# A block-sparse attention with a relu-squared layer on one core: SyncE's transfers wait for older ones from the third batch on, and one normalising changes places with two masks

## The chip, the core and the metric

The kernel runs on one core of a Trainium2 chip. Its time is the device time in microseconds of one execution; of several executions the median is given. The engines are TensorE (PE in the profile), VectorE (DVE), ScalarE (ACT), GpSimd (POOL) and SyncE (SP), which here only issues transfers. A core has 16 DMA engines, shared by all queues.

## The reference, cut to what matters

```python
batch, n_heads, seq, head_dim = 4, 8, 768, 64;  block = 32;  n_blocks = 24;  n_rand = 3
scores = (q @ k.T) / sqrt(64)                    # for each batch and head
mask = |blk_i - blk_j| <= 1  or  blk_i in (0, 23)  or  blk_j in (0, 23)
mask[rows of block qb, columns of block kb] = True   for kb in sampled_blocks[qb]
attn = softmax(where(mask, scores, -1e9))
x = (attn @ v) as [3072 tokens, 512]
out = relu(x @ w_in) ** 2 @ w_out                # w_in 512 x 2048, w_out 2048 x 512
```

Inputs and output are in float32; the kernel computes in bfloat16 with float32 sums.

## The kernel before, in words

The work is a list of small tasks, numbered in the order in which they are made, and a written-out order of them, `PROGRAM` (L1009). A word such as `V433` names the engine (V VectorE, P TensorE, A ScalarE, G GpSimd, S SyncE) and the task; `/2` behind a TensorE task is the PSUM buffer, one of four, that it takes. `run_program` (L96) goes through the words and emits each task. Every engine works off its own words in this order; between engines they wait for each other's data and buffers by semaphores. `HOLD` (L77) lets four gathers of GpSimd begin behind a named product.

A *unit* is a pair of heads of one batch: four units a batch, 16 in all. Batches 0 and 1 (units 0 to 7) are computed densely: scores of 256 queries against 256 keys at a time, `exp` on ScalarE (L364), a multiplication by the 0/1 mask on VectorE (`masks`, L371), the products with V (`values`, L376) and a normalising on VectorE (`normalize`, L410: a reciprocal, L414, and a multiplication, L417). The normalising reads the PSUM buffer in which the products with V were summed, and that buffer is free for other work when it is done.

Batches 2 and 3, the third and the fourth, (units 8 to 15) are computed sparsely, in six *visits* of four query blocks each. For a visit `k_gather` (L589) copies the sampled K blocks from the transposed K (`QKT`) into `KG`, on GpSimd or VectorE, and `v_gather` (L576) fetches the sampled V rows from a copy in DRAM into `VG`, with an indirect transfer of GpSimd or six small ones of SyncE; `v_window` (L547) fetches the neighbouring and the first and last V rows. The products with V come out of L660.

Around this run the transfers of SyncE, in the order of the S words: `load` (L151) brings a unit's q, k or v in float32 into SBUF (V at L155; Q and K of the third and fourth batch at L157, in rows of 512 bytes); a cast on GpSimd, VectorE or ScalarE; `transp_dma` (L318) turns the cast Q or K into `QKT` with a transposing transfer at L319; `v_store` (L539) writes V rows to DRAM for the gathers; `x_transp_dma` (L442) and `s_transp` (L672) transpose the normalised result into `xT`; `store` (L774) writes the output. SyncE works strictly in order: a transfer that has to wait for its data or its buffer holds all later ones.

The second layer, in tiles of 256 tokens, fills in between: `hidden` (x times w_in), `relu`, `square`, `output` (g times w_out), `out_copy`, `store`. Most matmuls are issued in pairs, for the two halves of the rows, by a helper at L209.

The place of the order that the change touches, around the end of the second batch, reads

```python
A903 P432 P906 P476/0 V418 P481/2 A477 S621 V412 V433 A482 V498 V541 G499 P914/1
V478 V483 P915 G503 P486/0 P419/2 ...
```

`P432` finishes the products with V of unit 7's last 256 queries, `V433` normalises them, `P914/1` (a `hidden` part) takes the PSUM buffer 1 that `P431/1` and `P432` had used. `V418` and `V412` are masks of unit 6, whose products are `P419` and `P420`. `P476` and `P481` are the first scores against gathered K blocks of the third batch; `V502`, ahead of all these V words, picks blocks with `k_gather`. `S435` transposes the normalised result of the second batch once all four units' are there.

Of the kernel before, what the change touches and what calls it, by code (L numbers as in the profile page):

```python
# [25 lines left out]
def kernel(  # L26
# [49 lines left out]
    AHEAD = {(2, 4, 9): 2, (3, 0, 1): 0}  # L76
    HOLD = {586: 976, 563: 977, 564: 978, 542: 956}  # L77
# [18 lines left out]
    def run_program(bufs):  # L96
# [81 lines left out]
    sy, sc_ = nc.sync, nc.scalar  # L178
# [772 lines left out]
    for us in [range(b * HP, (b + 1) * HP) for b in range(B)]:  # L951
        for u in us:
# [20 lines left out]
    for T in TILES:  # L973
# [34 lines left out]

    PROGRAM = """  # L1009
        V109 V153 V207 V332 V18 V19 V20 V28 V42 V53 V294 V29 A32 V35 P30/0 P36/1 V31 P0/2 V1 P2/3 P15/0 P33/2 G43 A3 V37 P100/0 V34  # L1010
        P84/1 G46 P104/3 G57 P88/2 V85 A101 V89 G54 P98/1 A105 P102/0 V99 P92/2 P47/3 P44/1 A103 V93 P9/2 A48 G41 P58/0 P94/2 P86/3
        A59 V45 P111/1 A87 V95 P113/0 P55/2 P106/3 V67 A112 A114 V56 G64 P68/1 P123/2 V107 P14/0 G74 V52 A69 P108 A124 G75 P115/1 G78
        S80 P90/0 V110 V91 P125/3 G63 A116 P121/2 P65/0 A122 P117/1 V66 G49 P82/0 A126 G70 P135/2 V118 P119 P131/3 G38 A136 V83 V60
        V120 P133/0 P61/2 V73 P127/1 V62 P174/2 A132 P50/3 A134 V128 A175 P171/0 P129 V51 V130 A172 P10/3 V176 P168/3 P11/1 P4/2
        P39/1 A169 V40 V173 P137/2 G22 P144/0 A145 P12/1 P5/1 V138 V170 P141/1 P139 P147/3 V140 A142 P71/0 P177/2 V146 A148 P158/1
        V72 V178 P781/0 V149 A159 P782 P179 V180 S251 G79 V160 P184/3 P783 V143 P784 G76 S252 A185 P187/1 P774/2 P775 P181/3 A188
        P776 P777 P161/1 V785 V189 P150/0 V186 A182 A778 V151 P788/3 A162 P155/2 P789 G786 P152 A156 V183 G780 P215/1 A216 V154 P790
        P212/0 V163 P791 V157 P190/2 A792 V787 P164/1 A213 V191 P795/3 G793 A779 V165 P796 S81 P209/0 G794 P192 P166 P797 V167 V193
        P798 A210 P824/1 V217 V214 S259 S260 V383 G77 P825 A799 P197/2 P194/0 P826 A198 G801 P827 P818/3 A195 V828 P819 G254 P226/2
        A800 P820 S255 V196 A227 P200/0 P812/1 V211 V264 P813 A201 S267 P243/2 P821 V256 S265 P814 A244 V228 P218/0 P815 V199 A822  # L1020
        P219 P802/2 A816 V220 S257 V202 P240/3 P221 P803 A241 V262 S261 P96/1 P804 A222 V97 A817 P237/3 V242 P223/0 P203/1 A238 S268
        V245 P805 S263 V272 A224 P229/3 P204 P806 A230 G266 S275 S276 P286/0 V225 A823 P807 S273 V231 A287 P808 V205 P232/3 A829 V270
        P206 P289/0 S271 P233 V239 V208 P809 A290 V234 V288 P296/1 S253 A810 P246/0 V291 S437 P235 P247 V236 A297 P299/2 V248 P830/3
        P831 A300 V280 P302/1 V278 P832 A303 P249 S279 P283/2 V250 P833 V298 A284 P852/0 V834 V434 P314/1 S277 P853 A315 S281 P846/2
        V304 P847 A835 V285 P311/3 P854 V258 P855 A312 V301 P848 S269 P849 V316 A856 P292/1 S21 V313 P864/3 A850 P293 P305/0 G282
        V295 P865 A857 P308/2 G851 S454 P306 S436 A309 P866 V307 P353/1 P867 A354 P326/0 V868 P858/2 G439 P859 A327 P320/1 P860 V274
        A321 P323/3 S438 V310 P836/0 S444 A324 V355 S460 P861 V322 P347/1 S445 P837 V496 A862 V328 V325 G441 P317/3 A348 P350/2 P318
        P838 S811 V319 A351 V349 P329/1 A869 P334/3 V352 P330 P839 V331 A335 V23 P356/2 G443 A863 P340/1 P840 S333 A341 P841 P362/3
        P357 G447 P842 A363 P337/1 P843 S452 A338 G459 S442 P870/3 G449 A844 P359/1 P871 S446 A360 V345 V342 V358 S440 V339 P374/0
        P872 A375 V336 P365/1 S450 P377/2 V361 P873 A366 V364 P343/0 S462 A378 V367 P371/1 P344 S845 P874 A372 S448 V346 V376 P368/2  # L1030
        P398/0 V373 P369 A399 P875 V379 S461 V370 P380/1 V470 S453 P401/0 P381 A402 P385/2 V382 P876 V400 A386 S384 P391/0 P16/1 P877
        V451 A392 V403 P404/1 P886/2 V878 A405 P887 P388/0 P425/1 A389 V406 P24/3 P888 V27 V25 A426 P889 P880/0 A890 P881 G463 P428/1
        P882 A429 G467 P883 V427 V26 S613 P407/2 G465 S631 A884 P408 S468 S469 A891 P892/1 P893 P422/3 G455 S464 V396 V409 P926/0
        V457 P927 P894 S456 P928 V390 A423 P929 P895 S466 A885 V424 P413/2 V387 A930 G471 V393 P898/3 A414 V896 P899 S458 P394/0 A931
        P900 V430 P395 S615 P416/1 A417 A897 P932/2 V397 P901 S605 P933 V902 V539 G473 P410/0 P431/1 P934 S614 A411 P935 V415 S472
        P904/3 A936 V502 P905 A903 P432 P906 P476/0 V418 P481/2 A477 S621 V412 V433 A482 V498 V541 G499 P914/1 V478 V483 P915 G503
        P486/0 P419/2 A487 P907 A937 P916 P491/0 P917 A492 P420 A918 P479/0 P908 V421 A480 S435 V488 P489/2 P920/1 V545 A490 P474/0
        G546 P909 A475 P484/2 V493 P910 S501 G616 A485 P911 G500 A919 P494/0 V912 G626 S913 P921 V519 V495 S544 P507/2 P7/3 P922 A508
        P513/3 P923 A514 G636 P948/2 G620 V582 P949 A924 V515 P510/0 P504/3 P950 V509 S623 A511 P951 G523 A505 P954/1 V952 P553/0
        A925 P955 S606 P938/3 V512 S622 P556/2 V506 P939 S879 A557 G524 P940 A554 S497 P956 G542 G543 P547/2 P957 A548 P941 V958 S617  # L1040
        P516/0 V549 V558 P525/2 V584 P550/1 V517 P942 A526 G588 A959 P943 S518 P944 A953 S522 P528/2 A551 P966/0 P967 A529 G520 V552
        S627 P945 V555 V530 G618 P960/1 A946 P968 P531/2 P961 A532 G608 P969 P962 S630 V970 G624 P534/3 P963 S609 A535 P559/2 G521
        V665 V533 A971 V589 S629 G566 V562 A964 P994/0 P995 S619 P988/3 V560 P989 G965 P996 V610 P990 P593/1 P997 A594 S561 P991 V536
        P972/2 A998 V992 G628 G585 P1000/1 S607 A999 P973 V527 V567 S611 S587 P590/0 P1001 A591 P974 P1002 S625 P1003 P537/3 A1004
        P982/0 V667 V538 A993 P983 G632 G612 P975 V634 A1005 S540 S633 P984 V595 P596/1 P976 G586 P568/3 P985 S635 A597 P977 G563
        V708 V986 A569 S565 P599/1 V598 P978 G564 S637 A600 S638 V601 P574/3 S947 P979 A575 P1022/0 A987 V980 P1023 P571/1 P1028/3
        A572 V592 S981 P1029 P1024 V573 P1025 V642 P577/2 P1030 P602/1 A578 G668 A1026 P1006/2 V639 V603 G640 A1027 P643/0 P1007 V570
        S604 G671 A644 P1008 V576 S641 V579 P655/1 P1031 A656 P1034/0 A1032 P1035 P1009 P648/1 P1036 A649 P1037 P580/3 A1038 P1010
        V710 V581 A1033 P645/1 P658/3 V672 P1011 S583 A659 P1012 A646 P650/0 P1016/3 V647 A651 P660/1 P1017 A661 P653/0 P1013 V662
        A654 V657 V652 P1018 V692 A1014 P1019 G693 P663/1 V751 A1020 S1015 A1039 P682/0 G1021 V664 P679/2 P1050/3 A680 S670 P1051  # L1050
        P1056/1 A683 P676/2 G669 V681 P1052 P1053 P1062/0 S666 A677 P1057 V1054 P1063 P1058 P673/2 P1064 A674 P1059 P1040/3 A1055
        V1060 P1065 P1068/2 V684 A1061 P1069 V675 P694/1 V678 P1041 A1066 V714 P1070 A695 P685/0 G715 A1067 P1071 V688 V753 V686
        P700/1 P1042 A1072 G1073 S687 P1043 A701 G689 P722/0 P697/2 P1044 A723 S712 V702 P703/1 P1045 A704 P716/0 A698 P1046 V735
        P725/1 A717 P1047 G736 P1090/2 A1048 V696 P1091 P1084/0 G690 A726 P1085 P719/3 P1092 A720 G757 S713 P1074/1 P1093 V758 P1086
# [42 lines left out]
```

## Time and profile before

| | |
|---|---|
| median of 3 runs | 258.28 us (256.19 to 260.79) |
| the profiled execution's own time | 257.4 us |
| its span in the profile | 255.6 us |
| granted clock of TensorE | 1.000 |
| DMA: bytes, mean rate over the span | 47.08 MB, 184 GB/s |
| of these on q1, SyncE's queue | 37.61 MB, 65.2% of the 16 engines' time |
| on q0, GpSimd's queue | 8.25 MB, 16.2% |

How to read it: the profile lists every instruction of one execution with its engine and its line in the kernel. A group's row names line, engine, operation, the buffers written and read (out<-in), how many there were and their busy time. In the timeline a row has start, length and, in square brackets, the engine's idle time before it with what ended it; "issue" stands for an end that no semaphore of the program explains. SPq is SyncE, which is never "busy": its rows tell how long it took to issue transfers. A row of the view by window has start:end, length, and then for each engine, in the order PE, PEld (weight loads of TensorE), DVE, ACT, POOL, the busy time and the number of instructions in brackets; then the granted clock, the DMA engines' share and the rate in GB/s. A row of a DMA queue has packets, MB and their time as a share of 16 engines over the window. A row of the view of waits has who waits for whom, the total in us, how often, and the longest.

### The profile page before, as it was taken

Reading aid. Unit: us, or ns where it says so; the run is one execution under the profiler, and the core shown is the slowest. Engines: PE = TensorE matmul, PEld = TensorE weight load, DVE = VectorE, ACT = ScalarE, POOL = GpSimd, SP = SyncE. Lnnn points to the kernel's source line nnn. Section 1 sums busy time; section 2 is a strip of 40 time slices with the busy share of each in tenths; the row PEclk is TensorE's granted clock in tenths of the full one; section 3 lists DMA queues with packets and bytes.
Section 4 is the critical chain, followed back from the end, with each engine's and each line's share of the span. In section 5 each row is a group of like instructions: output and inputs, shape, how many; then the busy total and the mean of one; then the engine's idle time right before and its main releaser. Section 6 shows DMA issues by size and latency. Waiting matters only on the chain.

```text
span 255.6 us, 12045 instructions
## 1 busy us (share of the span) xinstructions
PE 242.8 (95%) x5265; PEld 182.0 (71%) x5265; DVE 165.6 (65%) x386; ACT 184.8 (72%) x216; POOL 99.0 (39%) x200
## 2 busy tenths in 40 slices
PE   7998999999999989969999899899999999999994
PEld 4776888669865668857967676666975775776774
DVE  7779987799787878764654666526465478642300
ACT  3899999999998798948648476758697647225241
POOL 2674253010544015167466844144427406150020
PEclk9999999999999999999999999999999999999999
DMA  6999999999899999997799999983525654342022
GB/s 197 371 265 212 197 308 130 251 216 230 224 291 188 248 169 263 142 269 142 225 278 148 185 232 204 291 221 82 159 44 88 158 152 112 94 128 82 3 85 85
DMA packets 63540, 47.08 MB, mean 184 GB/s; under 512 B 31487, under 2 KB 58496, under 8 KB 63488
## 3 DMA queue, kind: packets, MB, share of 16 engines
q1 hardware_dynamic: 58352, 37.61, 65.2%
q0 software_dynamic: 4448, 8.25, 16.2%
q8 instruction: 41, 0.67, 1.2%
q10 hardware_dynamic: 688, 0.46, 0.6%
q14 instruction: 11, 0.09, 0.1%
HBM read 35.51 MB, written 7.91 MB: 170 GB/s over the span
## 4 chain that ended last, share of the span: by engine, by line
PE 81%; DVE 8%; DMA 5%; issue 2%; ACT 1%; DVEq 0%; POOL 0%; SPq 0%; ACTq 0%; POOLq 0%
PE X L209 73%; PE X L660 5%; DMA VG<-rows,idx 3%; DVE pT L371 2%; PE X L402 2%; DMA QKT<-qc 2%; ACT pT L364 1%; DVE r L716 1%; DVE VG L286 1%; DVE xq L417 1%; PE X L312 1%; DVE KG L604 0%; DVE VB L129 0%; DVE oh L238 0%; DVE rs L414 0%
## 5 line engine op out<-in xcount | busy, mean ns | idle before, releaser
L209 PE MATMUL X<-xT,w_in_sb 64*128 64x256 bf16 x1536 | 99.7, 269 | 3.1 <-DVE XS L417 2.0
L209 PE MATMUL X<-w_out_sb,g 64*128 64x512 bf16 (+3 forms) x960 | 94.5, 333 | 0.0
L209 PEld LDWEIGHTS <-w_in_sb 64*128 64x128 bf16 x1536 | 73.5, 94 | 16.0 <-issue 4.1
L364 ACT ACTIVATE pT<-X 128x1024 bf16<-128x1024 f32 x72 | 70.5, 1034 | 5.5 <-PE X L209 4.4
L630 ACT ACTIVATE pT<-X 128x768 bf16<-128x768 f32 (+1 forms) x56 | 41.5, 766 | 28.7 <-PE X L209 27.1
L209 PEld LDWEIGHTS <-g 64*128 64x128 bf16 x960 | 40.3, 94 | 26.2
L725 ACT ACTIVATE g<-r 128x1024 bf16<-128x1024 f32 (+1 forms) x43 | 39.6, 936 | 11.8 <-DVE r L716 11.7
L371 DVE TENSOR_TENSOR pT<-pT,VG 128x1024 bf16<-128x1024 bf16 x60 | 41.1, 720 | 2.4 <-ACT pT L364 0.9
L716 DVE TENSOR_SCALAR r<-X 128x1024 f32<-128x1024 f32 x21 | 25.7, 1223 | 24.6 <-PE X L209 23.0
L727 POOL TENSOR_TENSOR g<-r 128x512 bf16<-128x512 f32 (+1 forms) x16 | 21.2, 1338 | 50.0 <-DVE r L716 26.7
L714 ACT ACTIVATE r<-X 128x1024 f32<-128x1024 f32 x27 | 28.4, 1064 | 10.8 <-PE X L209 10.7
L637 DVE TENSOR_TENSOR pT<-pT,MKS 128x768 bf16<-128x768 bf16 (+1 forms) x48 | 27.4, 602 | 12.1 <-ACT pT L630 11.2
L209 PE MATMUL X<-QKT 64*128 64x256 bf16 (+1 forms) x384 | 32.8, 254 | 1.6 <-issue 0.8
L583 POOL DMA_INDIRECT VG<-rows,idx x20 | 20.4, 1019 | 25.7 <-PE X L209 12.2
L209 PEld LDWEIGHTS <-QKT 64*128 64x128 bf16 x384 | 17.4, 97 | 7.0 <-issue 2.4
L129 POOL CAST qc<-ks 128x384 bf16<-128x384 f32 (+1 forms) x18 | 10.0, 582 | 27.0 <-DMA ks<-in_k_dram 17.9
L129 POOL CAST VB<-vs 128x768 bf16<-128x768 f32 x10 | 9.7, 972 | 24.8 <-DMA vs<-in_v_dram 23.5
L209 PEld LDWEIGHTS <-pT 64*128 64x128 bf16 x768 | 15.7, 94 | 3.0 <-PE X L209 0.2
L209 PE MATMUL X<-VB,pT 64*128 64x65 bf16 x768 | 17.2, 190 | 0.1
L209 PEld LDWEIGHTS <-KG 64*128 64x128 bf16 x528 | 13.3, 95 | 4.4 <-POOL KG L604 0.3
L660 PEld LDWEIGHTS <-pT 128*64 128x64 bf16 x624 | 11.8, 111 | 5.2 <-issue 4.8
L209 PE MATMUL X<-QKT,KG 64*128 64x64 bf16 x528 | 15.0, 190 | 0.0
(107 smaller groups left out, 201.5 us busy)
## 6 DMA issues: line engine op xcount, KB each, us to landing
vs<-in_v_dram SPq DMA_DIRECT2D x14, 384.0 KB
ks<-in_k_dram SPq DMA_DIRECT2D x13, 384.0 KB
qs<-in_q_dram SPq DMA_DIRECT2D x12, 384.0 KB
out_dram<-ys SPq DMA_DIRECT2D x9, 512.0 KB
VG<-rows SPq DMA_DIRECT2D x20, 132.0 KB
w_in_sb<-in_moe_w_in_dram POOLq DMA_DIRECT2D x2, 1024.0 KB, 11.7
w_out_sb<-in_moe_w_out_dram POOLq DMA_DIRECT2D x4, 512.0 KB, 14.5
rows<-VB SPq DMA_DIRECT2D x4, 396.0 KB
```

The costliest lines, as they stand in the source:

```text
L129: (V if e == "DVE" else G).tensor_copy(out=out, in_=in_)
L209: last = nc.tensor.matmul(out(r ^ crossed), lhsT(r ^ crossed, rows), rhs(r ^ crossed, rows), skip_group_check=True, **kw)
L364: A.activation(out=pT[:, :, 0:n], in_=stile.pop(a)[:, :, 0:n], func=AF.Exp, scale=scale)
L371: V.tensor_tensor(out=pT, in0=pT, in1=m[:, None].broadcast_to([P, 2, len(cs), w]), op=AOP.mult)
L583: G.indirect_dma_start(out=to[0:RS * HB], out_offset=None, in_=pairs, in_offset=bass.IndirectOffsetOnAxis(ap=idx[0:RS * HB, g - 1:g], axis=0))
L630: A.activation(out=pT[:, :, 0:n], in_=stile.pop((u, v, gs))[:, :, 0:n], func=AF.Exp, scale=scale)
L637: V.tensor_tensor(out=pT, in0=pT, in1=m[:, None].broadcast_to([P, 2, n]), op=AOP.mult)
L660: nc.tensor.matmul(po[i * D:(i + 1) * D, h, a * VW:(a + 1) * VW], pts[g][:, h, c * D:(c + 1) * D], val, start=a == 0 and c == 0, stop=c == ...
L714: A.activation(out=to, in_=src, func=AF.Relu)
L716: V.tensor_scalar(out=to, in0=src, scalar1=0.0, scalar2=None, op0=AOP.max)
L725: A.activation(out=g, in_=r, func=AF.Square)
L727: (G if e == "POOL" else V).tensor_mul(out=g, in0=r, in1=r)
```

## The change

Two things change. First, SyncE's transfers go through a small class, `Paced`. It keeps for each transfer a name and a cost, the number of rows times (1000 + bytes in a row). From the first S word whose task belongs to the third batch or to anything made after it (`S437`, the load of unit 8's K, and with it all later S words, whatever their batch), each transfer first counts back from the youngest one sent: as long as the sum of costs stays within 1,900,000 they may be under way. If there is an older one that is not yet known to have landed, SyncE gets an instruction ahead of the transfer that does nothing but wait for the landing of the youngest of those. Transfers of GpSimd and ScalarE are not counted and do not wait. Second, in `PROGRAM` the word `V433` moves from behind `V412` to ahead of `V418`; all other words keep their order (the diff breaks the lines anew).

```diff
+    ROW_COST, UNDER_WAY = 1000, 1900000
...
             held_by[0] = passed.get(HOLD.get(int(i)))
+            sy.on = sy.on or (word[0] == 'S' and t in third)
             t.fn(names[word[0]])
...
-    sy, sc_ = nc.sync, nc.scalar
+    class Paced:
+        def __init__(self):
+            self.sent, self.landed, self.on = [], 0, False
+
+        def dma_start(self, out, in_, **kw):
+            row = (D * 2 if kw else in_.shape[-1]) * (4 if in_.dtype == F32 else 2)
+            cost = math.prod(in_.shape) // (D * 2 if kw else in_.shape[-1]) * (ROW_COST + row)
+            under_way, k = 0, len(self.sent)
+            while k > self.landed and under_way + self.sent[k - 1][1] <= UNDER_WAY:
+                k -= 1
+                under_way += self.sent[k][1]
+            if self.on and k > self.landed:
+                tc.add_manual_dep(nc.sync.nop().ins, self.sent[k - 1][0], SYNC, reason="little is under way when the next transfer begins")
+                self.landed = k
+            i = nc.sync.dma_start(out=out, in_=in_, **kw)
+            self.sent.append((i.ins.name, cost))
+            return i
+
+    sy, sc_ = Paced(), nc.scalar
...
     for us in [range(b * HP, (b + 1) * HP) for b in range(B)]:
+        if us[0] == SB * HP:
+            first = len(tasks)
         for u in us:
             prepare(u)
...
+    third = set(tasks[first:])
     PROGRAM = """
...
-        A903 P432 P906 P476/0 V418 P481/2 A477 S621 V412 V433 A482 V498
+        A903 P432 P906 P476/0 V433 V418 P481/2 A477 S621 V412 A482 V498
```

More of the change, by code (lines that the diff above doesn't have):

```diff
@@ L1013 @@
[L1013 to L1048, printed above, removed]
@@ L1061 @@
[L1061 to L1064 removed]
+        V109 V153 V207 V332 V18 V19 V20 V28 V42 V53 V294 V29 A32 V35 P30/0 P36/1 V31 P0/2 V1 P2/3 P15/0 P33/2 G43 A3 V37
@@ new lines @@
+        P100/0 V34 P84/1 G46 P104/3 G57 P88/2 V85 A101 V89 G54 P98/1 A105 P102/0 V99 P92/2 P47/3 P44/1 A103 V93 P9/2 A48 G41
+        P58/0 P94/2 P86/3 A59 V45 P111/1 A87 V95 P113/0 P55/2 P106/3 V67 A112 A114 V56 G64 P68/1 P123/2 V107 P14/0 G74 V52
+        A69 P108 A124 G75 P115/1 G78 S80 P90/0 V110 V91 P125/3 G63 A116 P121/2 P65/0 A122 P117/1 V66 G49 P82/0 A126 G70
+        P135/2 V118 P119 P131/3 G38 A136 V83 V60 V120 P133/0 P61/2 V73 P127/1 V62 P174/2 A132 P50/3 A134 V128 A175 P171/0
+        P129 V51 V130 A172 P10/3 V176 P168/3 P11/1 P4/2 P39/1 A169 V40 V173 P137/2 G22 P144/0 A145 P12/1 P5/1 V138 V170
@@ new lines @@
+        P200/0 P812/1 V211 V264 P813 A201 S267 P243/2 P821 V256 S265 P814 A244 V228 P218/0 P815 V199 A822 P219 P802/2 A816
+        V220 S257 V202 P240/3 P221 P803 A241 V262 S261 P96/1 P804 A222 V97 A817 P237/3 V242 P223/0 P203/1 A238 S268 V245
+        P805 S263 V272 A224 P229/3 P204 P806 A230 G266 S275 S276 P286/0 V225 A823 P807 S273 V231 A287 P808 V205 P232/3 A829
+        V270 P206 P289/0 S271 P233 V239 V208 P809 A290 V234 V288 P296/1 S253 A810 P246/0 V291 S437 P235 P247 V236 A297
+        P299/2 V248 P830/3 P831 A300 V280 P302/1 V278 P832 A303 P249 S279 P283/2 V250 P833 V298 A284 P852/0 V834 V434 P314/1
@@ new lines @@
+        P927 P894 S456 P928 V390 A423 P929 P895 S466 A885 V424 P413/2 V387 A930 G471 V393 P898/3 A414 V896 P899 S458 P394/0
+        A931 P900 V430 P395 S615 P416/1 A417 A897 P932/2 V397 P901 S605 P933 V902 V539 G473 P410/0 P431/1 P934 S614 A411
+        P935 V415 S472 P904/3 A936 V502 P905 A903 P432 P906 P476/0 V433 V418 P481/2 A477 S621 V412 A482 V498 V541 G499
+        P914/1 V478 V483 P915 G503 P486/0 P419/2 A487 P907 A937 P916 P491/0 P917 A492 P420 A918 P479/0 P908 V421 A480 S435
+        V488 P489/2 P920/1 V545 A490 P474/0 G546 P909 A475 P484/2 V493 P910 S501 G616 A485 P911 G500 A919 P494/0 V912 G626
@@ new lines @@
+        S913 P921 V519 V495 S544 P507/2 P7/3 P922 A508 P513/3 P923 A514 G636 P948/2 G620 V582 P949 A924 V515 P510/0 P504/3
+        P950 V509 S623 A511 P951 G523 A505 P954/1 V952 P553/0 A925 P955 S606 P938/3 V512 S622 P556/2 V506 P939 S879 A557
+        G524 P940 A554 S497 P956 G542 G543 P547/2 P957 A548 P941 V958 S617 P516/0 V549 V558 P525/2 V584 P550/1 V517 P942
+        A526 G588 A959 P943 S518 P944 A953 S522 P528/2 A551 P966/0 P967 A529 G520 V552 S627 P945 V555 V530 G618 P960/1 A946
+        P968 P531/2 P961 A532 G608 P969 P962 S630 V970 G624 P534/3 P963 S609 A535 P559/2 G521 V665 V533 A971 V589 S629 G566
@@ new lines @@
+        V562 A964 P994/0 P995 S619 P988/3 V560 P989 G965 P996 V610 P990 P593/1 P997 A594 S561 P991 V536 P972/2 A998 V992
+        G628 G585 P1000/1 S607 A999 P973 V527 V567 S611 S587 P590/0 P1001 A591 P974 P1002 S625 P1003 P537/3 A1004 P982/0
+        V667 V538 A993 P983 G632 G612 P975 V634 A1005 S540 S633 P984 V595 P596/1 P976 G586 P568/3 P985 S635 A597 P977 G563
+        V708 V986 A569 S565 P599/1 V598 P978 G564 S637 A600 S638 V601 P574/3 S947 P979 A575 P1022/0 A987 V980 P1023 P571/1
+        P1028/3 A572 V592 S981 P1029 P1024 V573 P1025 V642 P577/2 P1030 P602/1 A578 G668 A1026 P1006/2 V639 V603 G640 A1027
@@ new lines @@
+        P643/0 P1007 V570 S604 G671 A644 P1008 V576 S641 V579 P655/1 P1031 A656 P1034/0 A1032 P1035 P1009 P648/1 P1036 A649
+        P1037 P580/3 A1038 P1010 V710 V581 A1033 P645/1 P658/3 V672 P1011 S583 A659 P1012 A646 P650/0 P1016/3 V647 A651
+        P660/1 P1017 A661 P653/0 P1013 V662 A654 V657 V652 P1018 V692 A1014 P1019 G693 P663/1 V751 A1020 S1015 A1039 P682/0
+        G1021 V664 P679/2 P1050/3 A680 S670 P1051 P1056/1 A683 P676/2 G669 V681 P1052 P1053 P1062/0 S666 A677 P1057 V1054
+        P1063 P1058 P673/2 P1064 A674 P1059 P1040/3 A1055 V1060 P1065 P1068/2 V684 A1061 P1069 V675 P694/1 V678 P1041 A1066
@@ new lines @@
+        V714 P1070 A695 P685/0 G715 A1067 P1071 V688 V753 V686 P700/1 P1042 A1072 G1073 S687 P1043 A701 G689 P722/0 P697/2
+        P1044 A723 S712 V702 P703/1 P1045 A704 P716/0 A698 P1046 V735 P725/1 A717 P1047 G736 P1090/2 A1048 V696 P1091
+        P1084/0 G690 A726 P1085 P719/3 P1092 A720 G757 S713 P1074/1 P1093 V758 P1086 G711 A1094 P1096/3 P1097 P1087 A1095
+        P1098 S691 V1088 P1075 P1076 V705 S1049 V718 P1099 V721 P1102/2 V699 P1103 S754 V1100 P1077 P706/0 V727 A1101 P743/3
+        V707 P1078 A744 V724 P1104 S709 P762/0 P1105 A763 P728/3 A1089 P768/0 V731 S734 P1079 V729 A1106 P1080 V764 S730
@@ new lines @@
+        A769 G1107 P1081 P765/3 P737/2 P1108/0 A766 S756 V770 G732 V1082 A738 P1109 P746/3 P1110 G733 V739 V745 P1111 V767
+        A747 G755 P1132/2 P1118/1 P740/3 P1119 A741 P1133 P1120 V742 P759/3 P1121 V748 A760 P1112 V1122 P749/3 V761 P1134
+        V750 P1135 P1139/1 S752 V1136 P771/3 P1113 A1137 G1138 V772 P1140 S773 G1124 P1125/2 P1126 P1141 G1123 S1083 P1142
+        P1127 A1143 P1128 P1114 V1129 G1144 P1115 A1131 P1156/3 A1116 P1157 P1146/1 A1145 S1117 P1158 A1130 P1163/2 P1159
+        P1164 V1160 P1147 P1148 A1162 A1161 P1177/0 P1165 P1178 P1170/3 P1171 P1179 P1180 P1149 V1181 P1172 P1173 P1166
@@ L1065 @@
+        A1174 P1150 V1167 P1151 A1169 G1168 P1152 A1183 P1153 A1176 G1175 A1182 P1184/0 A1154 P1185 P1186 S1155 P1187
+        P1194/3 P1195 P1188 P1189 P1190 P1196 P1197 P1191 P1198 A1192 P1199 P1200 P1201 S1193 P1214/2 P1215 P1216 A1202
+        P1217 P1204/1 P1205 P1206 S1203 P1218 P1219 P1207 P1220 P1221 P1208 P1209 A1222 P1210 P1211 P8/0 S1223 P6/3 P13/2
+        P17/0 V1212 S1213
     """
```

34 lines of the change are left out of this document (15 added, 19 removed).

## The prediction

> **What bounds the kernel now.** I read the page first, then who the TensorE waits for, then the chain that ended last, then the queue of SyncE and the DMA queues one by one.
>
> ```profile
> PE 242.8 (95%) x5265; PEld 182.0 (71%) x5265; DVE 165.6 (65%) x386; ACT 184.8 (72%) x216; POOL 99.0 (39%) x200
> q8 instruction: 41, 0.67, 1.2%
> ```
>
> TensorE is busy for 95% of the span, so the kernel is bound by its matmuls, and a change to queues and order can only win idle time of that engine. How much there is, and where, the next two views say: busy time by stage, and TensorE's waits from 56 us, about where the new waits begin, to 175 us.
>
> ```profile
> 56.00:170.00 114.00, 108.49 (x2467) 82.03 (x2462) 79.69 (x195) 89.29 (x101) 48.29 (x101) 1.00 1.07 219
> 170.00:255.60 85.60, 82.02 (x1774) 59.47 (x1770) 39.39 (x89) 46.36 (x60) 28.82 (x55) 1.00 0.39 100
> PE X L209 <- DVE XS L417: 2.0, 1, 2.0
> PE X L209 <- issue: 1.8, 2, 1.0
> PE X L660 <- issue: 1.3, 2, 1.1
> ```
>
> In the first stage the DMA engines are full (share 1.07) and TensorE idles 114.00 - 108.49 = 5.51 us. In the second the DMA share is 0.39, and the 3.6 us of idle time are mostly the last stores. Of the 5.51 us, 2.0 + 1.8 + 1.3 = 5.1 us are in five waits: one for a normalising (L417) and four in which TensorE waits for nothing that the program shows ("issue"). So 5.1 us, 2.0% of the run, is all that can be won.
>
> The "issue" waits have a pattern. Here are three of them in the timeline, then the instructions between them (the third and the fifth column's counts, matmuls and weight loads), then how many were left when a fetch of instructions began on queue q8 (the packets below).
>
> ```profile
> 93.62 0.28 PE L209 MATMUL X<-QKT 64*128 64x256 bf16 x2 [0.81 <-issue]
> 146.04 0.28 PE L209 MATMUL X<-xT,w_in_sb 64*128 64x256 bf16 x1 [0.96 <-issue]
> 165.28 0.38 PE L660 MATMUL X<-VG,pT 128*64 128x65 bf16 x11 [1.12 <-issue]
> 93.60:104.51 10.91, 10.72 (x256) 9.18 (x255) 9.24 (x19) 9.71 (x11) 4.06 (x7) 1.00 1.10 240
> 104.51:146.02 41.51, 38.40 (x892) 29.50 (x892) 23.61 (x58) 28.12 (x35) 26.30 (x73) 1.00 1.01 200
> 146.02:152.68 6.66, 6.45 (x127) 4.91 (x127) 4.76 (x12) 4.37 (x5) 3.30 (x4) 1.00 1.27 222
> 152.68:165.26 12.58, 11.47 (x255) 8.23 (x255) 7.80 (x20) 9.36 (x12) 4.70 (x6) 1.00 1.16 249
> 90.35:93.60 3.25, 2.38 (x34) 1.52 (x31) 2.75 (x4) 3.15 (x4) 0.00 (x0) 1.00 0.78 66
> 143.41:146.02 2.61, 1.66 (x31) 1.24 (x25) 0.73 (x2) 0.01 (x1) 2.60 (x9) 1.00 1.29 114
> 238.45:247.70 9.25, 9.25 (x142) 6.40 (x140) 2.45 (x2) 4.24 (x6) 2.04 (x2) 1.00 0.12 46
> q8 instruction: 1, 0.02, 117.0%
> q8 instruction: 1, 0.02, 81.9%
> ```
>
> From stall to stall lie 511, 1784, 254 and 510 instructions: 2, 7, 1 and 2 times 256, short by 1 to 8 (waits on semaphores take places too). The 41 packets on q8 carry 0.67 MB, 16 KB each; 10,530 TensorE instructions over 41 packets are 257 a packet. So TensorE stalls where it reaches the end of what has been fetched. The packet that ends the stall at 93.62 us began in the window 90.30 to 90.40 and took 1.17 x 16 x 0.10 = 1.9 us; TensorE then had 65 instructions left, and 56 in the stall at 146.04 us. Where the DMA engines are nearly free (the second packet, in 238.40 to 238.50, 0.819 x 1.6 = 1.3 us) the fetch begins 282 instructions ahead. The full DMA stage delays the fetches, and the DMA engines are full of what SyncE issues.
>
> **The normalising.** V433 (L414, L417) goes ahead of the two masks V418 and V412 (L371) on VectorE, nothing else in the written-out order moves, and it issues no DMA. The chain of waits has the place:
>
> ```profile
> 103.35 4.99 DMA QKT<-qc
> 110.29 0.58 issue
> 110.87 1.29 DVE pT L371 x2
> 112.17 0.10 DVE rs L414
> 112.29 0.44 DVE XS L417
> 112.77 8.28 PE X L209 x188
> ```
>
> TensorE waits for the PSUM buffer that this normalising reads (its 2.0 us). Ahead of the masks the normalising runs at 110.87 instead of 112.17 and ends 1.29 us sooner, near 111.4 us. The masks end that much later than now, by 0.10 + 0.02 + 0.44 = 0.6 us, near 112.7. Their readers are the products of P419:
>
> ```profile
> 113.73 0.54 PE L209 MATMUL X<-VB,pT 64*128 64x65 bf16 x24
> ```
>
> With TensorE 1.29 us ahead these would begin at 112.4, so some 0.3 us of the gain is given back: **1.0 us is won** (bounds 0.6, if the masks' whole 0.6 us come to bear, and 1.3).
>
> **The waits of SyncE.** From S437 on every SyncE transfer first adds up the costs of the youngest ones; as soon as the sum passes 1.9 million it waits for the landing of the one that no longer fits. By the code's formula a transposing of Q or K costs 768 x 1256 = 0.96 million, a load of Q or K in the third and fourth batch 768 x 1512 = 1.16, a load of V 0.65, a store of 256 rows 0.78, half of a store of V rows 0.79. So at most one transposing plus something small counts as under way; two make 1.93. It does bind, as SyncE's timeline shows (with one row of the view by tile: shortest, median and longest issue of a transposing, in ns; and the GpSimd row that such a landing releases):
>
> ```profile
> 86.03 1.90 SPq L319 DMA_TRANSPOSE QKT<-qc  x1
> 87.99 2.00 SPq L157 DMA_DIRECT2D ks<-in_k_dram  x2
> 90.08 4.73 SPq L444 DMA_TRANSPOSE xT<-XS  x2
> 99.03 8.88 SPq L319 DMA_TRANSPOSE QKT<-qc  x4
> L319 SPq DMA_TRANSPOSE QKT<-qc x24: 1211/1326/4214, 41.8 to 158.0; - x24
> 95.21 0.96 POOL L129 CAST qc<-ks 128x384 bf16<-128x384 f32 x2 [13.00 <-DMA ks<-in_k_dram]
> ```
>
> The first of the two K loads at 87.99 us has landed only at 95.2, when GpSimd is released. The second would now wait until the transposing of 86.03 has landed (1.16 + 0.96 passes 1.9), and the xT transposings at 90.08 until the first load has, some 5 us later than they were issued. Behind a waiting SyncE stand all later loads, transposings, windows and stores. But the hardware holds SyncE too: an issue that takes 1.3 us in the median has taken up to 4.2. A wait that replaces a hold delays no data as long as the DMA engines keep work. At the pace of the last SyncE row, 4 x 0.96 million in 8.88 us, 1.9 million is an estimated 4.4 us of work. The waits themselves are some 0.1 us each on a sequencer that is idle anyway; where SyncE has no backlog (after 170 us, DMA share 0.39) they are over when it comes to them.
>
> What the lighter queue is worth, two bounds. Below: nothing, if a fetch waits no shorter. Above: all "issue" stalls, 3.1 us. I credit nothing for the 0.81 us at 93.62, because TensorE would only arrive earlier at the K blocks of the third batch (the chain's 4.99 us, landing at 108.3 us), which come no sooner. Of the other 2.3 us I take about two thirds, **1.5 us**, because the fetch in the quiet stage started 282 instructions ahead and only some 100 would do. The block gathers of GpSimd gain too:
>
> ```profile
> DMA to landing us min/median/max: 3.5/6.1/8.5
> DMA to landing us min/median/max: 3.6/3.9/4.8
> 132.88 8.54 DMA VG<-rows,idx
> 141.46 0.89 PE X L660 x43
> ```
>
> They take 6.1 us in the median from 100 to 170 us and 3.9 from 170 to 225. I put this at nothing in the sum: the longest, 8.54 us, now ends just when TensorE wants it (141.42 against 141.46), and shorter gathers only keep the gains from being lost there.
>
> What it costs: the K blocks of the third batch.
>
> ```profile
> 108.46 0.30 DVE L598 COPY KG<-QKT 128x256 int32<-128x256 int32 x1 [1.02 <-DMA QKT<-qc]
> 108.46 0.54 POOL L598 COPY KG<-QKT 128x256 int32<-128x256 int32 x1 [1.72 <-DMA QKT<-qc]
> 110.16 0.64 PE L209 MATMUL X<-QKT,KG 64*128 64x64 bf16 x12
> ```
>
> Their transposings are issued from 99.03 us on, out of loads and casts of the crowded stage. VectorE and GpSimd are idle until they land, and in the written-out order TensorE's first products on KG come at 110.16, right behind the picking. So each microsecond that they come late is lost whole. Bounds: 0.8 us sooner (no better than the stall ahead of it allows) and 4.99 us later (one more landing in series). I take **0.2 us later**, near the lower end, since the waits mostly replace holds.
>
> Sum on the profiled execution (257.4 us, span 255.6 and 1.8 around it): 257.4 - 1.0 - 1.5 + 0.2 = 255.1. It lies 0.9 us under the median of the runs shown, 258.28; between the two bases I take **255.5 us**, about 1% less.
>
> [...]
>
> **Rivals.** (a) The K blocks come late and the kernel is slower. Place: 108 to 111 us. With two transposings allowed, the last of the third batch's K waits for one more landing, and all behind it move by up to the 4.99 us of the chain's row: 257.4 + 4.99 - 1.0 = 261.4 us, or 259.9 if the fetches still give their 1.5. From a delay of 2.5 us on (1.0 + 1.5) it outweighs the gains. For it: VectorE and GpSimd idle on exactly this landing. Against: SyncE is held just as long by the hardware now.
>
> [...]
>
> (c) The waits change nothing, since the hardware's own hold paces as tightly: 257.4 - 1.0 = 256.4 us. For it: issues of several us. Against: the two transfers at 88 and 90 us went out ahead of landings at 95.
>
> (d) All five waits vanish, the K blocks sooner by 0.8: 257.4 - 5.1 = 252.3 us.
>
> **How the numbers follow.** Forecast 50%, (a) 18%, (b) 14%, (c) 10%, (d) 8%. A measurement tells about 2% from no change, 253.1 to 263.4 us. Below 253.1 lie (d) and the lucky edge of the forecast, 0.15; above 263.4 only the worst of (a) on a slow basis, 0.05; the rest is 0.80. The range goes from (d), 252.3, to (a) with its fetches gained, 259.9 and a little, 260.2; the forecast's own is 253.8 to 257.0.
>
> **What would show it.** Right: TensorE's wait for L417 falls from 2.0 to about 0.7 us; of the "issue" waits after 100 us at most 1 us is left; the fetches of q8 begin more than 120 instructions ahead; gathers before 170 us have a median near 4.5; SyncE's single issues no longer take 3 to 4 us. Wrong: TensorE idles before the first products on KG near 110 us for more than 1 us (a); "issue" waits stay near 2 us with SyncE waiting (b), or with SyncE's issues unchanged (c); or new waits of TensorE for windows, gathers or xT after 115 us, which I have put at nothing.

## The result, and the profile after

The changed kernel takes 276.62 us (median of 4 runs, 275.12 to 278.48) against 258.2 us of the kernel before beside it (256.19 to 260.79): 1.0745 times as long, with a 95% interval of 1.0643 to 1.0846. It is 7.5% slower; 255.5 us was predicted, with a range to 260.2. Its profiled execution takes 276.39 us (before: 257.4), with a span of 274.3 us (255.6). The comparisons here and below leave disturbed runs out, so a ratio can differ a little from that of the two medians beside it.

First the busy time of the engines on the page of the kernel after, with the chain that ended last by engine; below it the chain of the kernel before:

```profile
PE 248.4 (91%) x5265; PEld 186.9 (68%) x5265; DVE 169.5 (62%) x386; ACT 184.9 (67%) x216; POOL 98.1 (36%) x200
...
PE 51%; DMA 26%; DVE 10%; SPq 5%; issue 3%; ACT 2%; another core or an unknown queue 1%; POOL 0%; DVEq 0%; POOLq 0%; ACTq 0%
```

```profile
PE 81%; DVE 8%; DMA 5%; issue 2%; ACT 1%; DVEq 0%; POOL 0%; SPq 0%; ACTq 0%; POOLq 0%
```

The span has grown by 18.7 us. TensorE is busy for 248.4 - 242.8 = 5.6 us more and idle for 274.3 - 248.4 = 25.9 us instead of 255.6 - 242.8 = 12.8, which is 13.1 us more. A quarter of the chain is now transfers (26%, before 5%). Who TensorE waits for from 56 to 200 us, in the kernel after (us in total, times, longest); in the kernel before, the three rows in the prediction are all there are:

```profile
PE X L229 <- DMA xT<-XS: 8.8, 3, 5.0
PE X L680 <- DMA VG<-rows: 2.3, 2, 1.3
PE X L229 <- DMA QKT<-qc: 2.2, 1, 2.2
PE X L229 <- DVE XS L437: 1.4, 1, 1.4
PE X L680 <- issue: 1.1, 2, 0.6
PE X L229 <- POOL KG L624: 0.5, 1, 0.5
PE X L229 <- ACT pT L650: 0.5, 1, 0.5
PE X L229 <- issue: 0.3, 1, 0.3
```

(After the change, L417 has become L437, L209 L229, L660 L680 and L598 L618. Every transfer of SyncE now has L194, and the waits ahead of them L192.) The "issue" waits have fallen from 3.1 to 1.4 us, as hoped. But 13.3 us of waiting for transfers stand where there was none: for transposed inputs of the output projection (xT), for window rows (VG) and for transposed Q and K (QKT).

The stages by window, the kernel before and then the kernel after:

```profile
56.00:130.00 74.00, 70.92 (x1667) 55.07 (x1662) 55.97 (x139) 63.10 (x71) 28.98 (x67) 1.00 1.02 215
130.00:195.00 65.00, 62.53 (x1392) 45.56 (x1390) 37.17 (x101) 45.97 (x55) 31.38 (x62) 1.00 0.87 176
165.00:195.00 30.00, 29.68 (x671) 21.60 (x673) 15.75 (x50) 22.84 (x28) 12.41 (x29) 1.00 0.52 127
```

```profile
56.00:130.00 74.00, 63.43 (x1388) 48.46 (x1380) 53.77 (x130) 56.31 (x62) 21.48 (x48) 0.95 0.80 178
130.00:195.00 65.00, 58.31 (x1226) 43.89 (x1226) 33.93 (x85) 39.23 (x48) 31.25 (x71) 0.97 0.90 193
165.00:195.00 30.00, 27.85 (x577) 19.62 (x572) 14.76 (x47) 20.07 (x26) 10.21 (x24) 1.00 0.95 189
102.40:109.20 6.80, 3.40 (x34) 2.83 (x36) 3.42 (x7) 0.36 (x1) 3.11 (x7) 0.50 0.62 155
136.50:139.90 3.40, 3.32 (x50) 2.90 (x52) 0.00 (x0) 1.08 (x2) 0.72 (x4) 0.50 0.87 276
```

In the stage that was full, the DMA share falls from 1.02 to 0.80 and the rate from 215 to 178 GB/s: in 74 us 2.7 MB less are moved, although as much is there to be moved. That work turns up later: from 165 to 195 us the share is 0.95 where it had been 0.52. TensorE gets through 1388 matmuls instead of 1667 up to 130 us. The last two rows are the two stretches in which its granted clock is 0.50. At full speed their 6.7 us of matmuls would have taken an estimated 3.4, so 3.4 of the 5.6 us of added busy time come from there; the other 2.2 I can't place.

How the transfers follow each other shows in the chain of waits of the kernel after around 100 us (start, length, what):

```profile
83.26 4.07 DMA qs<-in_q_dram
...
87.81 5.22 DMA QKT<-qc
...
93.05 0.02 SPq L192
...
93.10 4.04 DMA vs<-in_v_dram
...
97.16 0.02 SPq L192
...
97.20 4.66 DMA ks<-in_k_dram
...
101.92 1.20 SPq L194
...
103.16 2.50 DMA xT<-XS
...
105.80 6.26 PE X L229 x99
...
112.05 3.87 DMA QKT<-qc
```

Transfer after transfer is issued as soon as another has landed (0.02 us for the waiting instruction, 0.06 to 0.07 us from the landing to the next issue), and takes 2.5 to 5.2 us to land itself. On this chain they stand in series. SyncE's timeline and one row of VectorE's tell what that does to the loads and transposings followed in the prediction:

```profile
97.20 3.76 SPq L194 DMA_DIRECT2D ks<-in_k_dram  x2
101.92 2.50 SPq L194 DMA_TRANSPOSE xT<-XS  x2
```

```profile
116.96 0.29 DVE L618 COPY KG<-QKT 128x256 int32<-128x256 int32 x1 [1.52 <-DMA QKT<-qc]
```

The two K loads, issued from 87.99 us before, go out from 97.20; the xT transposings from 101.92 instead of 90.08; the last K block of the third batch is picked at 116.96 instead of 108.46 us, 8.5 us late. TensorE had already stopped for xT from 100.76 to 105.80 us:

```profile
105.80 4.44 PE L229 MATMUL X<-xT,w_in_sb 64*128 64x256 bf16 x48 [5.04 <-DMA xT<-XS]
```

By the trace's semaphore events the lateness grows: 14 us for a transfer that landed at 115 us (129 after), 20.2 us for an xT transposing that landed at 172.3 (192.5).

### The profile page after: what moved, and what is told of

The parts are those of the page before. It is cut to its first block, busy times and chain, and to the rows that moved or that the text cites. A ratio compares the mean times of both kernels' runs of the same rounds, so it can differ in the third digit from the quotient of the medians.

```text
span 274.3 us, 12089 instructions
## 1 busy us (share of the span) xinstructions
PE 248.4 (91%) x5265; PEld 186.9 (68%) x5265; DVE 169.5 (62%) x386; ACT 184.9 (67%) x216; POOL 98.1 (36%) x200
## 4 chain that ended last, share of the span: by engine, by line
PE 51%; DMA 26%; DVE 10%; SPq 5%; issue 3%; ACT 2%; another core or an unknown queue 1%; POOL 0%; DVEq 0%; POOLq 0%; ACTq 0%
PE X L229 45%; DMA QKT<-qc 7%; DMA xT<-XS 6%; DMA qs<-in_q_dram 5%; SPq L194 5%; DMA vs<-in_v_dram 5%; DVE pT L391 4%; PE X L680 3%; PE X L422 2%; DMA ks<-in_k_dram 2%; DMA VG<-rows 2%; ACT pT L384 1%; ACT pT L650 1%; PE X L332 1%
## 5 line engine op out<-in xcount | busy, mean ns | idle before, releaser
L229 PE MATMUL X<-xT,w_in_sb 64*128 64x256 bf16 x1536 | 102.7, 275 | 11.9 <-DMA xT<-XS 8.8
L229 PE MATMUL X<-w_out_sb,g 64*128 64x512 bf16 (+3 forms) x960 | 94.5, 333 | 0.0
L229 PEld LDWEIGHTS <-w_in_sb 64*128 64x128 bf16 x1536 | 76.5, 96 | 24.7 <-issue 8.3
L650 ACT ACTIVATE pT<-X 128x768 bf16<-128x768 f32 (+1 forms) x56 | 41.3, 763 | 39.3 <-PE X L229 36.4
L229 PEld LDWEIGHTS <-g 64*128 64x128 bf16 x960 | 40.5, 94 | 25.9
L391 DVE TENSOR_TENSOR pT<-pT,VG 128x1024 bf16<-128x1024 bf16 x60 | 41.9, 733 | 2.4 <-ACT r L734 1.2
L657 DVE TENSOR_TENSOR pT<-pT,MKS 128x768 bf16<-128x768 bf16 (+1 forms) x48 | 29.1, 636 | 14.4 <-ACT pT L650 13.1
L229 PE MATMUL X<-QKT 64*128 64x256 bf16 (+1 forms) x384 | 32.4, 254 | 3.3 <-DMA QKT<-qc 2.2
L229 PEld LDWEIGHTS <-QKT 64*128 64x128 bf16 x384 | 17.0, 97 | 9.2 <-issue 4.7
L131 POOL CAST VB<-vs 128x768 bf16<-128x768 f32 x10 | 8.5, 853 | 28.7 <-DMA vs<-in_v_dram 28.0
L229 PEld LDWEIGHTS <-KG 64*128 64x128 bf16 x528 | 14.1, 96 | 5.4 <-POOL KG L624 0.8
L229 PEld LDWEIGHTS <-pT 64*128 64x128 bf16 x768 | 15.5, 94 | 3.3 <-DVE pT L391 0.4
L680 PEld LDWEIGHTS <-pT 128*64 128x64 bf16 x624 | 12.4, 111 | 7.6 <-issue 4.9
L229 PE MATMUL X<-VB,pT 64*128 64x65 bf16 x768 | 17.1, 190 | 0.2
L680 PE MATMUL X<-VG,pT 128*64 128x65 bf16 x528 | 13.6, 197 | 3.6 <-DMA VG<-rows 2.3
```

Of the source, the lines that this page charges most:

```text
L131: (V if e == "DVE" else G).tensor_copy(out=out, in_=in_)
L229: last = nc.tensor.matmul(out(r ^ crossed), lhsT(r ^ crossed, rows), rhs(r ^ crossed, rows), skip_group_check=True, **kw)
L391: V.tensor_tensor(out=pT, in0=pT, in1=m[:, None].broadcast_to([P, 2, len(cs), w]), op=AOP.mult)
L650: A.activation(out=pT[:, :, 0:n], in_=stile.pop((u, v, gs))[:, :, 0:n], func=AF.Exp, scale=scale)
L657: V.tensor_tensor(out=pT, in0=pT, in1=m[:, None].broadcast_to([P, 2, n]), op=AOP.mult)
L680: nc.tensor.matmul(po[i * D:(i + 1) * D, h, a * VW:(a + 1) * VW], pts[g][:, h, c * D:(c + 1) * D], val, start=a == 0 and c == 0, stop=c == ...
```

## The experiments

The theory: 1.9 million of cost is too little to keep the DMA engines at work, since a transfer takes 4 us or more from issue to landing even when few are under way (4.04 to 5.22 us in four of the six of the chain above). Rivals: the waiting instructions themselves are dear; the moved normalising does harm; TensorE's halved clock is what costs. A last question was whether a wider limit wins anything over the kernel before. Each run is compared with the kernel before of its own series: 258.25 us for the first four, 255.44 for the next four, 254.91 for the last four. The ranges in the expectations were set for a kernel before of about 258 us, so in the two later series the ratio has to be held against them and not the time.

**The new order without the waits** (*order_only*).

```diff
-    ROW_COST, UNDER_WAY = 1000, 1900000
+    ROW_COST, UNDER_WAY = 1000, 1000000000000
```

> The normalising ahead of the two masks, no waits of SyncE. If the waits starve the DMA engines (theory), or if they cost by themselves (first rival), this lies where the kernel before lies, 256 to 259 us, with TensorE's wait for L437 near 0.7 us instead of 2.0. If the moved normalising is what costs (second rival), it lies above 270 us.

Measured: 257.07 us, ratio 0.9959 [0.9903, 1.0015]. The moved normalising isn't the cause. TensorE's waits from 56 us on:

```profile
PE X L229 <- issue: 3.0, 4, 1.7
PE X L680 <- issue: 1.7, 2, 1.1
```

The wait of 2.0 us for the normalising is gone (0.7 was expected), but the "issue" waits are 4.7 us instead of 3.1.

**The waits without the new order** (*waits_only*).

```diff
-        A903 P432 P906 P476/0 V433 V418 P481/2 A477 S621 V412 A482 V498
+        A903 P432 P906 P476/0 V418 P481/2 A477 S621 V412 V433 A482 V498
```

> All waits with the sum of 1.9 million, the normalising where it was. Theory and first rival: 275 to 279 us, as the changed kernel or 1 us above it. Second rival: 256 to 260 us.

Measured: 277.27 us, 1.074 [1.0638, 1.0843]: the whole loss. TensorE waits longer still for xT than with both edits (12.8 us in three waits), and 2.8 us for the normalising.

**Twice the limit, and four times** (*window_3M8*, *window_8M*).

```diff
-    ROW_COST, UNDER_WAY = 1000, 1900000
+    ROW_COST, UNDER_WAY = 1000, 3800000
```

and the same line with 8000000.

> The changed kernel with twice the sum, 3.8 million: 88 waits as before, but three or four transfers under way instead of one or two in the crowded stage. Theory: the DMA engines always have work, 256 to 260 us. First rival (each wait costs by itself, whatever it waits for): 272 to 278 us, since the number of waits is the same.

> The changed kernel with a sum of 8 million: 87 waits, each for a transfer that is eight or more back and should have landed. Theory: 256 to 259 us. First rival: 272 us or more.

Measured: 256.02 us, 0.9936 [0.9894, 0.9979], and 256.45 us, 1.0062 [1.0019, 1.0106]. Both have as many waiting instructions as the changed kernel, or one fewer (88 and 87 by the costs in the code; the profiles list 34 and 41 of them at L192, against 37 in the changed kernel), and the loss of 18 us is gone: the waiting instructions aren't dear, the number of transfers left under way decides. The two intervals lie on either side of no change, and that of 3.8 million didn't come again (below), so neither is read as a gain or a loss. The stage from 56 us for 8 million, then for 3.8 million:

```profile
56.00:130.00 74.00, 71.76 (x1681) 55.21 (x1676) 57.92 (x136) 62.09 (x70) 29.12 (x68) 1.00 1.08 230
```

```profile
56.00:130.00 74.00, 72.44 (x1689) 55.35 (x1687) 58.72 (x139) 63.24 (x72) 29.62 (x68) 1.00 0.97 219
```

With 3.8 million the rate is that of before. In this execution the DMA share is a little lower (0.97; in *window_3M8_again* it is 1.04), and TensorE waits less for what no semaphore explains. Its waits there:

```profile
PE X L680 <- issue: 1.9, 4, 0.5
PE X L229 <- DVE XS L437: 1.0, 1, 1.0
PE X L229 <- issue: 0.3, 1, 0.3
```

**A limit between** (*window_2M8*, the same line with 2800000).

> The changed kernel with a sum of 2.8 million: two or three transfers under way besides the new one, where 1.9 million left one or two and 3.8 million three or four. Theory (issue to landing takes some 4 us however few are under way, so the number under way sets the pace): between the two, 257 to 265 us. A rival in which 1.9 million hits one badly placed wait and the pace as such does not matter: 255 to 257 us, as with 3.8 million.

Measured: 257.02 us against 255.44, 1.0059 [0.9937, 1.0182]. The interval, which rests on two of the ten executions, takes in no change and a loss of 1.8%, so the time doesn't decide between the theory and the rival. In the profile, of an execution of 257.2 us where this kernel's fastest took 252.32, the same loss seems to begin, smaller by far than at 1.9 million: a wait for xT returns and the rate is 206 GB/s. Its waits, then its stage:

```profile
PE X L229 <- DMA xT<-XS: 1.9, 1, 1.9
PE X L229 <- DVE XS L437: 1.4, 1, 1.4
PE X L229 <- POOL KG L624: 1.2, 1, 1.2
```

```profile
56.00:130.00 74.00, 69.17 (x1584) 53.27 (x1581) 52.77 (x134) 60.07 (x68) 26.24 (x60) 0.98 0.92 206
```

**Where the loss arises** (*waits_to_S472* with the waits from S437 up to S472 alone, 31 of the 88; *waits_from_S472* with the other 57).

```diff
-            sy.on = sy.on or (word[0] == 'S' and t in third)
+            sy.on = (sy.on or word == 'S437') and word != 'S472'
```

```diff
-            sy.on = sy.on or (word[0] == 'S' and t in third)
+            sy.on = sy.on or word == 'S472'
```

> The changed kernel with waits only from S437 up to the word before S472 (31 of the 88), the stretch from 56 us to the K blocks of the third batch. The changed kernel's K was 8 us late there and its transfers 13 to 15 us late by S472. If this stretch makes the loss: 268 to 272 us. If the loss is made in the later stretch: 257 to 260 us.

> The changed kernel with waits only from S472 on (57 of the 88). If the early stretch makes most of the loss: 258 to 266 us, the remainder of 276.6. If both stretches lose alike, about 266 us each; if this one makes it: 270 us or more.

Measured: 266.45 us, 1.0477 [1.0332, 1.0621], and 262.35 us, 1.0312 [1.0126, 1.0499]. Together 7.9%, near the 7.5% of the whole. The first stretch, up to the third batch's K blocks, loses more by these two medians, but the intervals overlap; the loss isn't there alone, and the limit costs in both stretches. In the second case TensorE waits for xT again:

```profile
PE X L229 <- DMA xT<-XS: 5.9, 2, 4.8
```

**Every transfer waits for the one before** (*window_0*, the same line with 0). It measures the disputed quantity, the time from issue to landing with nothing else of SyncE's under way.

> The changed kernel with a sum of 0: from S437 on every transfer waits until the one before it has landed. Theory (most of the time from issue to landing is fixed): a lone transposing or load still takes 2.5 to 3.5 us, 85 of them up to the end of the crowded stage some 260 us, and the run lies at 380 to 450 us. Rival (the time from issue to landing is mostly queueing behind other transfers, so that alone it falls to the 1.3 us at which they land one after another in the kernel before): 280 to 310 us.

Measured in one execution: 458.24 us (span 456.2). That is even above what the theory gave, and far above the rival in which the time of a transfer shrinks with the load. The chain of waits shows the lone transfers, and the profile's strip of the DMA engines from 125 to 140 us (40 slices of 0.375 us) what they do meanwhile:

```profile
127.89 2.67 DMA out_dram<-ys
...
130.62 2.75 DMA QKT<-qc
...
133.44 3.40 DMA ks<-in_k_dram
```

```profile
DMA  0084992000999300008970000438960000274992
```

The transposing issued at 130.62 moves data in three slices from the 19th on ("897", from 131.75 us), and the next transfer's first data come at 134.4. On either side of its data lie four slices of zeros, 1.5 us, in which the engines have nothing. Over the whole run a lone transposing of Q or K took 2.75 us in the median, a load of 384 KB 3.1 (V) to 3.5 (Q, K), an xT transposing 2.4. By the packets in the trace the larger part of the time without data lies ahead of it: the medians of these four kinds are 1.0 to 1.2 us from issue to the first packet, and 0.3 to 0.5 us from the end of the last packet to the landing.

The same 27 transfers (24.15 million of cost, those that the kernel before issues from about 72 to 109 us) can be followed through all runs by their issue and semaphore events; "others" is how many more of SyncE's were under way when one was issued, on average, and the time that the 27 take runs from the landing of the transfer before them to that of the last:

| limit | others under way | issue to landing, mean | the 27 take | pace, million/us | time / before beside it, us |
|---|---|---|---|---|---|
| 0 | 0 | 3.1 us | 85.4 us | 0.28 | 458.2 / 255.4 |
| 1.9 million | 1.4 | 4.2 | 51.1 | 0.47 | 276.6 / 258.2 |
| 2.8 million | 2.4 | 5.0 | 44.5 | 0.54 | 257.0 / 255.4 |
| 3.8 million | 2.9 | 4.9 | 39.1 | 0.62 | 256.0 / 258.3 |
| 8 million | 3.3 | 5.2 | 37.5 | 0.64 | 256.5 / 258.3 |
| kernel before | 3.4 | 5.4 | 37.1 | 0.65 | |

Most of the time to landing is there already when a transfer is alone (3.1 of 5.4 us). So the pace hangs on how many are under way, and it is full only with about three others: the other runs in which no wait falls on these 27 have 0.62 to 0.63, so that 0.62 at 3.8 million isn't below them. At the full pace 1.9 million is 1.9 / 0.65 = 2.9 us of work, less than the 3.1 us that these transfers take to land on average even alone. The theory's 4 us or more holds from 1.4 others on, not for a transfer alone.

**Does the wider limit win anything?** (*window_3M8_again*; *window_3M8_old_order*, 3.8 million with V433 back behind V412; *order_only_again*.)

> The sum of 3.8 million once more, in more rounds, beside the two runs that each have one of its parts. Theory (a wide window starves nothing, keeps SyncE's queue from growing longer than that, and so lets TensorE's instruction fetches begin sooner; the normalising gives 1 us): 254 to 257 us, 0.3 to 1.2% under the kernel before. Rival (the gain of the first time was noise, or came from the normalising alone): not told apart from the run with the order alone.

> The wait with 3.8 million alone, the normalising behind the two masks as in the kernel before. If the wide window is what gains: about 1 us above the run with both, 255 to 258 us, and under the kernel before. If the normalising alone gains: as the kernel before, within 0.3%.

> The normalising ahead of the masks alone. By the prediction's term 1.0 us (0.4%) under the kernel before, bounds 0.6 to 1.3; with a ratio of 0.996 again the term holds, with 1.000 it is given back elsewhere.

Measured: 253.55, 254.57 and 254.56 us, each median of 12, against 254.91: ratios 1.0 [0.9959, 1.0041], 0.9995 [0.9937, 1.0052] and 0.9997 [0.9958, 1.0037]. The 0.6% of the first *window_3M8* didn't come again. No version is measurably faster than the kernel before.

**Is it the halved clock?** (*kept_warm*: the changed kernel, with 36 and 14 pairs of matmuls on constant data ahead of the hidden layer's two parts that waited longest for xT; their products go nowhere, since the real ones start the sum anew.)

```diff
+            for _ in range({(1, 256, 8): 36, (1, 512, 0): 14}.get((b, c0, f), 0)):
+                pair(lambda i: htile[T, f][:, i, 0:w], lambda i, rows: warm[rows, 0:P], lambda i, rows: warm[rows, 0:w], start=True, stop=True)
```

> The changed kernel with 36 idle pairs of matmuls ahead of the product that waits 5.0 us for xT near 106 us and 14 ahead of the one that waits 2.3 us near 136.6 us; they write a PSUM buffer that the real products then overwrite. In the changed kernel the granted clock is at half for 6.8 us from 102.4 us and for 3.4 us from 136.5 us. If the half clock behind these two waits adds to the loss: clock 1.0 there and 272 to 275 us. If the late transfers alone set the time, so that slow matmuls only fill what would be waiting: clock 1.0 there and 276 to 278 us.

Measured: 273.35 us, 1.075 [1.0661, 1.0839], the same loss. (The time alone would lie in the first range; by the ratio, on the base of 258.2 us, it is 277.6 and lies in the second.) The clock does stay at 1.00 where the dummies run, and falls elsewhere:

```profile
100.00:110.00 10.00, 9.82 (x216) 8.52 (x211) 4.98 (x9) 5.53 (x7) 3.59 (x7) 1.00 0.82 177
120.70:124.10 3.40, 3.40 (x54) 2.53 (x51) 1.47 (x4) 1.44 (x2) 2.18 (x7) 0.50 1.15 332
130.00:140.00 10.00, 10.00 (x264) 8.30 (x262) 5.51 (x8) 5.73 (x8) 4.99 (x14) 1.00 0.95 185
171.90:178.70 6.80, 2.81 (x36) 2.40 (x38) 0.00 (x0) 0.57 (x1) 1.35 (x2) 0.50 0.99 160
```

The wait for xT has only moved, to one of 6.1 us that ends at 175.9 us:

```profile
PE X L229 <- DMA xT<-XS: 6.3, 2, 6.1
```

The half clock lasts 10.2 us in all, as in the changed kernel, so this run doesn't show what it would cost if it could be kept off everywhere. What bounds it is the view by window: the matmuls in the changed kernel's two slow stretches took 3.4 us more than at full speed, so the clock accounts directly for at most 3.4 of the 18.7 us. That the slow stretches fill time in which TensorE would have waited for transfers anyway is likely, but not shown.

## Why the prediction was wrong

**What bounds the kernel now** isn't contradicted: 5.1 us was all that could be won, and no run won a measurable part of it that came again in a second series.

**The step that failed** is "A wait that replaces a hold delays no data as long as the DMA engines keep work", with the 4.4 us put beside it. The condition was the right one, its estimate wrong twice over. The pace came from four transposings that SyncE issued in 8.88 us (0.43 million/us), a row in which SyncE itself was held; measured over a long stretch it is 0.65. And the estimate was held against nothing: the time from issue to landing, which decides whether 2.9 us of work are enough, stood in the rows (the chain's 4.99 us; a K load issued at 87.99 that released GpSimd at 95.21) and wasn't compared with it. Even the 4.4 us would have lain under the 5.4 us of the kernel before.

**The hold of the hardware isn't a wait at 1.9 million.** "The hardware holds SyncE too" was true, up to 4.2 us an issue, but it came with 3.4 others under way on average. The limit leaves 1.4. The wait replaced nothing; it came on top.

**The K blocks**: "0.2 us later, near the lower end", with an upper bound of "4.99 us later (one more landing in series)". They came 8.5 us late. One more landing in series was too little because 88 of the 136 transfers from S437 on have a wait of their own, and the delays add up.

**The new waits for windows, gathers or xT**, "put at nothing", are the largest item: 8.8 us for xT and 2.3 for window rows. They were named as what would prove the forecast wrong. Rival (a) had the right mechanism and the right condition, at a quarter of the price: at most 261.4 us, since it looked at one place, 108 to 111 us, where all later transfers fall behind as well. Rivals (c) and (d) are out by the time itself.

**The landings** are heard of late, but not by much: the lone transposing of *window_0* takes 2.75 us from issue to landing, about 1.1 us of it ahead of the data, 1.1 with data and 0.5 behind, so that a wait for it hears of the end of the data some 0.5 us late.

**The fetches of instructions**: the prediction had the stalls right, and the runs show it more sharply than its rows did. Counted from the start of the program, these stalls come at the same instructions in every run that has them, here ahead of TensorE's number 6064 (matmuls and weight loads, 3032 each) in the kernel before and in *window_3M8_again*:

```profile
0.00:146.02 146.02, 138.09 (x3032) 106.34 (x3032) 111.38 (x260) 121.90 (x138) 61.84 (x137) 1.00 1.04 223
0.00:144.80 144.80, 138.13 (x3032) 106.84 (x3032) 115.71 (x263) 121.81 (x138) 60.63 (x137) 1.00 1.06 227
```

The others come at 3769, 4280, 4791, 5301, 6318 and 6828. The "issue" waits that are left in the kernel after (1.4 us, at 5553, 5558 and 5972) are not among them, and waits like these shift from run to run (5551 to 5609, 5972 to 5988), so their cause seems to be another one, which stays open. The stalls at the fixed numbers have gone from 3.1 us to nothing, where the sum had counted on 1.5. But this doesn't show that a shorter queue alone ends them: with 3.8 million they come to 0, 2.8 and 2.3 us in three profiles, with no waits to 3.1, 3.1 and 3.7, and with 1.9 million TensorE also waits 13.3 us for transfers, which would give the fetches time (this is not shown). So outcome (b), that the fetches wait as long as before, is out for 1.9 million and close to what two of the three profiles at 3.8 show. In the total no gain can be told at any limit.

**The normalising**: its wait was 2.0 us, and 1.4 in the kernel after, where it is late itself:

```profile
119.99 0.18 DVE L434 RECIPROCAL rs<-X 128x4 f32<-128x4 f32 x1 [1.20 <-ACT pT L650]
```

VectorE waits there for the exponentials of ScalarE (L650). In *order_only* the wait is gone, as predicted, and the total still stays within 0.4% of before. A microsecond can't be told there; whether it was won and lost again to the longer "issue" waits stays open. Nor is the move needed for a short wait: in *window_3M8_old_order*, with V433 back behind the masks, it is 0.2 us, against 1.0 and 0.9 with the move.

**The smaller signs came true**: the fetches ahead of six of the fixed numbers (all but 5301) begin 154 to 256 instructions ahead (48 to 209 in the kernel before, counted in the same way), gathers have a median of 4.5 us (here from 100 to 190 us), and no issue of a transposing takes more than 2.4 us:

```profile
DMA to landing us min/median/max: 3.7/4.5/8.4
```

```profile
L194 SPq DMA_TRANSPOSE QKT<-qc x24: 1210/1238/2365, 40.9 to 175.1; - x24
```

Before, the gathers had a median of 6.1 us and an issue took up to 4.2. I take the last two to mean that the DMA queues have become shorter, and they would look like a success to someone who read only them.

## What to carry to other kernels

A limit on transfers under way has to cover the time from issue to landing times the pace that the stage needs; here that is an estimated 5 us times 0.65 million/us, about 3.3 million, and 3.8 million cost nothing that could be measured where 1.9 cost 18 us. The estimate is on the safe side, since the limit leaves out the transfer about to be sent (0.9 million on average of the 27); where between 1.9 and 3.8 million the loss begins isn't measured, as the run with 2.8 can't be told from no change. Read both from the profile before a limit is set: the landing times from the chain or the releases, the pace over a stretch of many transfers and not from a row in which the queue is held. A transfer ahead of its need is not idle cover to be trimmed: shorter queues, quicker issues and quicker gathers came with a run that was 7.5% slower.

## What the hardware showed that I had not expected

- Of a transposing's 2.75 us alone, the engines move data for only about 1.1 us; about 1.1 us lie ahead of it and 0.5 behind. Issue to landing goes from 3.1 us with nothing else of SyncE's under way to 4.2 with 1.4 others and 5.4 with 3.4.
- TensorE's stalls at the end of what has been fetched come at the same instructions in every run that has them (3769, 4280, 4791, 5301, 6064, 6318, 6828). The distances are 511, 511, 510, 763, 254 and 510; with the waiting instructions of its sequencer counted too, they are 512, 512, 512, 768, 256 and 512. How long each takes (0 to 1.8 us) changes from one execution to the next.
- TensorE's clock was halved behind idle times of 1.1 to 5.0 us. In the kernel after it was idle from 100.76 to 105.80 us, the half clock began near 102.4 and lasted 6.8 us; after the idle time from 134.26 to 136.58 it began near 136.5 and lasted 3.4 us. An idle time of 2.21 us that ended at 68.5 us brought none, while in *kept_warm* the half clock at 120.7 us came behind idle times of 1.1, 1.2 and 1.5 us with matmuls between them; so the length of one idle time doesn't decide it. The half clock began 1.6 and 2.2 us into the two idle times of the kernel after, and each of the four stretches shown (102.4 and 136.5 us there, 120.7 and 171.9 in *kept_warm*) lasted 3.4 or 6.8 us.
